# Causal attention and a gated linear unit on one core: every engine's queue ordered by a list schedule written into the kernel, the first batch loaded pair by pair

## The chip, the cores and the metric

The kernel runs on one core of a Trainium2 chip. A core has five instruction queues that run beside each other and wait for one another on semaphores: PE (matrix products and transposes), DVE (vector work), ACT (exponentials, tanh, copies), POOL (a slower vector engine) and SP (which here only issues DMA transfers). The metric is the device time of one execution in microseconds. Three runs of the kernel before took 287.56, 288.27 and 291.65 us, median 288.27.

## What is computed

```
scores = q @ k.T / 8                      # 8 batches, 8 heads, 576 positions, 64 wide
cum    = cumsum(max(s, 0))                # per head, over positions
scores = causal(scores + min(cum[key] - cum[query], 0))
x      = softmax(scores) @ v              # heads side by side: 576 x 512 per batch
gate   = sigmoid(sum over 5 shifts of conv_w[k] * shifted x)    # per channel
out    = (gate * (x @ w_val)) @ w_out
```

The causal mask makes the decay a product of a factor of the query and a factor of the key, so the kernel multiplies the key's factor into v once (the tile `Vp`) instead of adding a bias to every score. A ones column beside v gives the softmax's sum.

## The kernel before

The unit of work is a **pair**: two heads of one batch, 32 pairs in all, four to a batch. For each batch:

- SP loads q and k (`load_qk`, L260, 1 MB each), the last 64 positions of both (`tail`, L268) and v (`load_v`, L330, five blocks into the one buffer `vst`).
- POOL converts q, k and tail to bf16 (L262, L270) and multiplies v by the decay factor `w` (L332, five instructions). For batch 0 alone the conversions are DVE's.
- PE transposes tail (L343) and, per pair, q and k (L353, 8 transposes); ACT copies the results out of PSUM into `QKT` (L344, L354).

For each pair: three groups of score products (L359, masks added by L396) with an exponential on ACT after each (L397); 30 products with `Vp` into the one PSUM buffer `psav` (`av`, L409); a reciprocal and a multiply on DVE (L417, L418, "norm"); five transposes of the result on PE (L429) and a copy to `xT` on DVE (L430); the convolution on DVE as five instructions per pair, "taps" (L437 the first, L439 the other four); tanh on ACT (L441). For each batch then eight products with w_val (`val`, L451), each with a DVE multiply by the gate (L453, "glu"), and five products with w_out (`outp`, L461), each with a copy on ACT (L464) and a store (L465). A short check of the reciprocals on DVE (L552 to L555) ends in a count that every engine reads.

Score groups take turns on two PSUM buffers; transposes, val, outp and the conversion of conv_w (L488, L489, to the tile `cwT` that all taps read) share two more, `m`.

What sets the order: `fills(n)` lists the work besides the scores that pair n brings (the next batch's transposes among it), half of the waiting list is emitted after every two score groups, and the build's own scheduler then moves instructions within each queue. At the start w_val and w_out are loaded after v, and POOL converts them (L481).

## Time and profile before

| | us |
|---|---|
| three runs | 287.56, 288.27, 291.65 |
| the profiled execution | 286.0 |
| its span, first to last instruction | 284.2 |
| DVE busy | 215.8 (76%) |
| PE busy | 208.3 (73%) |
| ACT busy | 175.5 (62%) |
| POOL busy | 108.6 (38%) |

The busy shares are means over a span with different limits. At the start the engines wait for the first loads and conversions, in the middle DVE is busy nearly all the time, and at the end PE and ACT finish the last two batches' products while DVE has little left. "Busy" counts the time in which at least one instruction of the engine was under way. A wait is put down to the event that came last.

### The profile page before, as it was taken

How to read it: one execution, taken by the hardware profiler on the slowest of the kernel's cores; microseconds unless marked ns; L12 is line 12 of the kernel's file. 1: busy time of each engine (PE TensorE's matmuls, PEld its weight loads, DVE VectorE, ACT ScalarE, POOL GpSimd, SP SyncE). 2: the span in 40 equal slices, each digit the busy share in tenths (PEclk: the TensorE clock that was granted, in tenths of full speed). 3: DMA queues.
4: the chain of work that ended last, by engine and by line, in shares of the span. 5: the costliest groups of instructions: out<-in, count | busy, mean ns of one | idle time of the engine just before them, and what ended most of it. 6: DMA issues, size and time to landing. Idle time of an engine off the chain costs nothing. (4 is left out here: it accounts for less than half of the span.)

```text
span 284.2 us, 6148 instructions
## 1 busy us (share of the span) xinstructions
PE 208.3 (73%) x2534; PEld 135.4 (48%) x2555; DVE 215.8 (76%) x342; ACT 175.5 (62%) x218; POOL 108.6 (38%) x87
## 2 busy tenths in 40 slices
PE   0779285468859977587878967798689898774990
PEld 0547263247534744464555634564366556442540
DVE  4303229997999799949997799949995999999310
ACT  1389264756564867587648866795659887622250
POOL 9379976940691046602490229201810000000000
PEclk9999869567995999999959999999989999997996
DMA  6997999999410029955868486501100201210342
GB/s 171 292 293 234 256 261 240 273 241 281 115 38 0 2 88 246 267 88 131 258 201 174 120 267 157 127 21 74 40 37 17 80 37 40 92 39 37 129 161 76
DMA packets 69054, 40.49 MB, mean 142 GB/s; under 512 B 46933, under 2 KB 63317, under 8 KB 69018
## 3 DMA queue, kind: packets, MB, share of 16 engines
q1 hardware_dynamic: 69018, 40.01, 52.6%
q8 instruction: 22, 0.36, 0.6%
q14 instruction: 14, 0.11, 0.1%
HBM read 30.57 MB, written 9.44 MB: 141 GB/s over the span
## 5 line engine op out<-in xcount | busy, mean ns | idle before, releaser
L439 DVE SCALAR_TENSOR_TENSOR gp<-xT,cwT,gp 128x576 f32<-128x576 bf16 x128 | 126.2, 992 | 0.6
L397 ACT ACTIVATE P<-ps 128x1024 bf16<-128x1024 f32 x96 | 94.5, 1024 | 19.8 <-PE ps L359 11.2
L332 POOL TENSOR_TENSOR Vp<-vst,w 128x520 bf16<-128x520 f32 x40 | 55.2, 1405 | 31.6 <-PE psav L409 25.9
L359 PE MATMUL ps<-QKT 64*128 64x128 bf16 (+4 forms) x576 | 49.3, 259 | 16.7 <-ACT P L397 15.1
L409 PE MATMUL psav<-Vp,P 128*128 128x65 bf16 x960 | 45.0, 201 | 11.1 <-DVE xn L418 10.9
L262 POOL CAST qkb<-qkf 128x2048 bf16<-128x2048 f32 x14 | 28.6, 2046 | 58.1 <-PE m L353 27.2
L409 PEld LDWEIGHTS <-P 128*128 128x128 bf16 x960 | 38.5, 102 | 22.4 <-issue 16.7
L461 PE MATMUL m<-wo,glu 128*128 128x512 bf16 x139 | 40.2, 396 | 11.7 <-DVE glu L453 9.5
L451 PE MATMUL m<-xT,wv 128*128 128x288 bf16 x256 | 41.3, 299 | 9.0 <-ACT ot L464 6.3
L441 ACT ACTIVATE th<-gp 128x576 f32<-128x576 f32 x32 | 21.9, 686 | 34.5 <-DVE gp L439 34.1
L359 PEld LDWEIGHTS <-QKT 64*128 64x128 bf16 x576 | 23.6, 99 | 39.0 <-issue 31.5
L464 ACT COPY ot<-m 128x512 f32<-128x512 f32 (+1 forms) x40 | 23.3, 582 | 22.8 <-PE m L461 10.6
L354 ACT COPY QKT<-m 128x1024 bf16<-128x1024 bf16 x32 | 31.4, 1019 | 5.6 <-PE m L353 5.6
L451 PEld LDWEIGHTS <-wv 128*128 128x128 bf16 x256 | 24.1, 101 | 21.6 <-issue 15.1
L453 DVE SCALAR_TENSOR_TENSOR glu<-th,m 128x288 bf16<-128x288 f32 x64 | 28.6, 447 | 5.5 <-PE m L451 5.5
L430 DVE COPY xT<-m 128x576 bf16<-128x576 bf16 x32 | 14.5, 452 | 24.0 <-PE m L429 23.0
L461 PEld LDWEIGHTS <-glu 128*128 128x128 bf16 x160 | 15.5, 99 | 27.1 <-issue 14.6
L353 PE MATMUL m<-ident,qkb 128*128 128x128 bf16 x256 | 22.5, 244 | 5.5 <-ACT QKT L344 2.5
L418 DVE TENSOR_TENSOR xn<-psav,recs 128x640 bf16<-128x640 f32 x32 | 26.2, 818 | 0.3
L437 DVE TENSOR_SCALAR gp<-xT,cwT 128x576 f32<-128x576 bf16 x32 | 24.7, 771 | 1.8
L353 PEld LDWEIGHTS <-qkb 128*128 128x128 bf16 x256 | 18.9, 110 | 9.0 <-issue 6.6
L417 DVE RECIPROCAL recs<-psav 128x10 f32<-128x10 f32 x32 | 6.8, 212 | 15.9 <-PE psav L409 15.9
(52 smaller groups left out, 118.2 us busy)
## 6 DMA issues: line engine op xcount, KB each, us to landing
vst<-in_v_dram SPq DMA_DIRECT2D x32, 256.0 KB, 5.5
out_dram<-ot SPq DMA_DIRECT2D x32, 256.0 KB, 2.0
qkf<-in_q_dram SPq DMA_DIRECT2D x7, 1024.0 KB, 6.8
qkf<-in_k_dram SPq DMA_DIRECT2D x7, 1024.0 KB, 8.5
tail<-in_q_dram SPq DMA_DIRECT2D x8, 128.0 KB, 7.8
tail<-in_k_dram SPq DMA_DIRECT2D x8, 128.0 KB, 6.9
vst<-in_v_dram SPq DMA_DIRECT2D x8, 128.0 KB, 5.0
qkf<-in_moe_w_val_dram SPq DMA_DIRECT2D x1, 1024.0 KB, 6.5
```

The source lines that it names most:

```text
L262: cast(t.rearrange("p j (h d) -> p h j d", h=8)[:, h0:h1], f.rearrange("p h (j d) -> p h j d", j=4)[:, h0:h1])
L332: nc.gpsimd.tensor_tensor(Vp[:, i], vst[:, i], w[:, i, b * 8:(b + 1) * 8].unsqueeze(2).to_broadcast([128, 8, 65]), ALU.mult)
L353: nc.tensor.transpose(pt[:, which, j * 128:(j + 1) * 128], st["qk"][which][:, j, c], ident)
L354: nc.scalar.copy(st["QKT"][:, :, p, 0:512].rearrange("d w (x j) -> d w x j", j=4), pt.rearrange("d w (j x) -> d w x j", j=4))
L359: nc.tensor.matmul(ps[:, hh, c0:c0 + nq], st["QKT"][r, 1, p, k0:k0 + 128], st["QKT"][r, 0, p, q0:q0 + nq], **kw)
L397: nc.scalar.activation(out=st["P", p][:, :, step * 512:(step + 1) * 512], in_=ps, func=AF.Exp, scale=0.125)
L409: nc.tensor.matmul(psav[:, hh, qb * 65:qb * 65 + 65], lhsT, Vp[:, kb, 2 * p + hh, :], start=(kb == 0), stop=(kb == qb))
L418: nc.vector.tensor_tensor(st["xn"][:, :, p * 128:(p + 1) * 128].rearrange("t g (h d) -> t h g d", h=2), pv[:, :, :, 0:64], rec.unsqueeze(3 ...
L439: nc.vector.scalar_tensor_tensor(gp, xc[:, kk:kk + S], cwT[:, c, kk:kk + 1], gp, ALU.mult, ALU.add)
L451: nc.tensor.matmul(psv, wv[:, dc, c * 128:(c + 1) * 128], st["xT"][:, dc, 4 + o:4 + o + 288], start=(dc == 0), stop=(dc == 3))
L453: nc.vector.scalar_tensor_tensor(st["glu"][:, c, o:o + 288], st["th", c][:, o:o + 288], 1.0, psv, ALU.add, ALU.mult)
L461: nc.tensor.matmul(pso, st["glu"][:, c, WIN[i]:WIN[i] + 128], wo[:, c, :], start=(c == 0), stop=(c == 3))
```

## The change

Nothing that is computed changes, and nearly every instruction exists before and after in the same shape. What the change does:

- **Order.** The kernel's code first lists every piece of work as a task with an engine, a cost, a due time (the table `DUE`, relative to the pair's number), the tasks it depends on and the buffers it takes and gives. `Plan.run` then steps through time and gives each free engine the ready task with the earliest due time. The tasks are emitted in that order, and the build's scheduler is told to keep it.
- **First batch.** q and k of batch 0 come pair by pair into their own buffers instead of two parts; v of batch 0 in twelve transfers (two per pair of 128 KB and one of 32 KB) instead of five. The conversion of k is ACT's (four of 128x512), that of q DVE's (four of 128x512). The four multiplications of v by the decay factor are DVE's.
- **Weights.** w_val and w_out are converted by DVE instead of POOL, and are loaded after q and k of batch 1, w_out later than those of batch 2.
- **v of later batches.** POOL multiplies by pair (four instructions of 128x650) instead of by block (five of 128x520).
- **Buffers.** Each buffer is one tile with one name; the plan gives out the numbers. There are six `th` buffers instead of five, and q's and k's bf16 tiles have two each instead of three in common.

```diff
+DUE = dict(av=1.09, norm=1.14, xt=0.4, xe=-1.97, tap=1.69, dtap=0.24, tanh=1.19, cpe=-13.67, val=4.62,
+           dval=0.22, out=9.31, dout=0.72, oute=4.54, qt=-4.04, qe=-3.19, tt=-2.41, te=-5.83, s4=-0.87,
+           vp=-4.81, cast=-10.12, lqk=-10.71, lv=4.53)
...
+            for e in engs:
+                if idle_at[e] > now + 1e-9:
+                    nxt.append(idle_at[e])
+                    continue
+                pick = None
+                seen = 0
+                for t in todo[e]:
+                    at = ready_at(t)
+                    seen += 1
+                    if seen > 60:
+                        break
+                    if at is None:
+                        continue
+                    if at > now + 1e-9:
+                        nxt.append(at)
+                        continue
...
+    t_wvo = []
+    for nm, src, dst, sc, key in (("wv", moe_w_val, wv, 1.0, -5), ("wo", moe_w_out, wo, 0.5, -2.4)):
+        def load(nm=nm, src=src):
+            wt = slot[nm] = work("qkf", nm, [128, 4, DM], FP32)
+            nc.sync.dma_start(out=wt, in_=src.rearrange("(c p) d -> p c d", c=4))
+        t = add("SP", 3.6, key, load, take=[("qkf", nm)])
+        t_wvo.append(add("DVE", 1.35, key + 7, lambda nm=nm, dst=dst, sc=sc: nc.vector.tensor_scalar(
+            dst, slot[nm], sc, None, ALU.mult), [t], give=[("qkf", nm)]))
+    t_wv, t_wo = t_wvo
...
+    t = add("SP", 0.3, -1, lambda: nc.sync.dma_start(out=cw, in_=moe_conv_w))
+    t = add("PE", 0.3, 0, conv_T, [t], take=[("m", "cw")], mode="N")
+    t_cw = add("DVE", 0.15, 0.1, lambda: nc.vector.tensor_copy(cwT, slot["cw"]), [t], give=[("m", "cw")])
...
+    def vprime(eng, b, p):
+        h = slice(2 * p, 2 * p + 2)
+        eng.tensor_tensor(Vps[b % 2][:, :, h], vst[:, :, h],
+                          w[:, :, b * 8 + 2 * p:b * 8 + 2 * p + 2].unsqueeze(3).to_broadcast([128, NKB, 2, 65]),
+                          ALU.mult)
+
+    def load_v_pair(p):
+        for h in (2 * p, 2 * p + 1):
+            nc.sync.dma_start(out=vst[:, 0:4, h, 0:64], in_=v[0, h, 0:512, :].rearrange("(i p) d -> p i d", i=4))
+        nc.sync.dma_start(out=vst[64:128, 4, HP[p], 0:64],
+                          in_=v[0, HP[p], 512:576, :].rearrange("h s d -> s h d"))
...
-    def load_v(b):
...
-            nc.gpsimd.tensor_tensor(Vp[:, i], vst[:, i],
...
+            t_tl = add("SP", 1.6, -8.4, lambda: load_tail(0))
+            t_tail = T["tailc", 0] = add("DVE", 0.45, -6, lambda: nc.vector.tensor_copy(tailbs[0], tails[0]), [t_tl])
+            for p in range(4):
+                for wh in range(2):
+                    def ld(p=p, wh=wh):
+                        f = slot["f", 0, wh, p] = one.tile([128, 2, 256], FP32, name=f"first{p}{wh}")
+                        dma_qk(0, wh, HP[p], f)
+                    t = add("SP", 0.95, -8.5 + 0.5 * p + wh * 0.01, ld)
+                    T["cast", 0, wh, p] = add(("DVE", "ACT")[wh], (0.32, 0.5)[wh], p - 9, lambda p=p, wh=wh: cast_qk(
+                        (nc.vector.tensor_copy, nc.scalar.copy)[wh], 0, wh, HP[p], slot["f", 0, wh, p]), [t])
+                t = add("SP", 1.4, -8.3 + 0.5 * p, lambda p=p: load_v_pair(p))
+                T["vp", 0, p] = add("DVE", 0.85, p - 2, lambda p=p: vprime(nc.vector, 0, p), [t, t_w])
...
+                t = add("SP", 3.8, n0 + DUE["lqk"], ld, take=[("qkf", (b, wh))])
+                c = add("POOL", 1.95, n0 + DUE["cast"], lambda b=b, wh=wh: cast_qk(
+                    nc.gpsimd.tensor_copy, b, wh, slice(0, 8), slot["f", b, wh]),
+                    [t] + [T.get(("qt", b - 2, p)) for p in range(4)], give=[("qkf", (b, wh))])
...
+                T["vp", b, p] = add("POOL", 1.4, n0 + p + DUE["vp"], lambda b=b, p=p: vprime(nc.gpsimd, b, p),
+                                    ts + [t_w, T.get(("av", b - 2, p))])
...
-        nc.gpsimd.tensor_scalar(dst, wt, sc, None, ALU.mult)
...
+    plan.total = plan.run()
+    with tc.manual_schedule():
+        for t in plan.order:
+            t["emit"]()
```

The start on DVE, from the first batch's last two norms to the first tap (`psav` and `xn` are the norm, `xT` the copy after PE's transposes, `cwT` the convolution's weights, `gp` the taps). Before:

```order
L418 TENSOR_TENSOR xn<-psav,recs 128x2x5x64
L489 COPY cwT<-m 128x20
L417 RECIPROCAL recs<-psav 128x10
L418 TENSOR_TENSOR xn<-psav,recs 128x2x5x64
L417 RECIPROCAL recs<-psav 128x10
L418 TENSOR_TENSOR xn<-psav,recs 128x2x5x64
L430 COPY xT<-m 128x576
L437 TENSOR_SCALAR gp<-xT,cwT 128x576
L439 SCALAR_TENSOR_TENSOR gp<-xT,cwT,gp 128x576
```

and with the change:

```order
L599 TENSOR_TENSOR xn_116<-psav,recs 128x2x5x64
L611 COPY xT_118<-m_502 128x576
L598 RECIPROCAL recs<-psav 128x10
L599 TENSOR_TENSOR xn_116<-psav,recs 128x2x5x64
L454 TENSOR_SCALAR wv<-qkf_176 128x2048
L477 COPY cwT<-m_614 128x20
L618 TENSOR_SCALAR gp_628<-xT_118,cwT 128x576
L611 COPY xT_118<-m_622 128x576
L621 SCALAR_TENSOR_TENSOR gp_628<-xT_118,cwT,gp_628 128x576 x4
```

The conversion of w_val (`wv`) now stands between the last norm of batch 0 and the copy that makes `cwT`, and three of batch 0's four copies to `xT` have moved ahead of it; before, all of them stood behind the four norms.

On PE the weights of the convolution are transposed from `cw`. With the change, behind the first two score groups of batch 1 (`QKT_113` is batch 1's, `xn_116` holds the norms of batch 0):

```order
L537 MATMUL s_607<-QKT_113 128x448
L537 LDWEIGHTS QKT_113
L537 MATMUL s_607<-QKT_113 128x448
L461 MATMUL m_614<-identf,cw 128x5 x4
L607 LDWEIGHTS xn_116
L607 MATMUL m_622<-ident,xn_116 128x128
L607 LDWEIGHTS xn_116
```

Before, that transposition stood between two products of batch 0 with `Vp`:

```order
L409 MATMUL psav<-Vp_162,P 128x65
L409 LDWEIGHTS P
L409 MATMUL psav<-Vp_162,P 128x65
L488 MATMUL m<-identf,cw 128x5 x4
L409 LDWEIGHTS P
L409 MATMUL psav<-Vp_162,P 128x65
L409 LDWEIGHTS P
```

So it moved from batch 0's attention to behind batch 1's transposes and two of its score groups.

The end on DVE: glu are the multiplies by the gate, `ok` and `okm` the check. Before:

```order
L439 SCALAR_TENSOR_TENSOR gp<-xT,cwT,gp 128x576 x4
L453 SCALAR_TENSOR_TENSOR glu<-th,m 128x288
L439 SCALAR_TENSOR_TENSOR gp<-xT,cwT,gp 128x576
L453 SCALAR_TENSOR_TENSOR glu<-th,m 128x288
L439 SCALAR_TENSOR_TENSOR gp<-xT,cwT,gp 128x576
L552 TENSOR_SCALAR ok<-recs 128x320
L553 SCALAR_TENSOR_TENSOR ok<-recs,ok 128x320
L555 TENSOR_REDUCE okm<-ok 128x1
L453 SCALAR_TENSOR_TENSOR glu<-th,m 128x288 x8
L560 CAST okcnt<-m 1x1
```

With the change:

```order
L621 SCALAR_TENSOR_TENSOR gp_3777<-xT_119,cwT,gp_3777 128x576
L651 SCALAR_TENSOR_TENSOR glu_121<-th_3725,m_3799 128x288
L651 SCALAR_TENSOR_TENSOR glu_121<-th_3779,m_3805 128x288
L621 SCALAR_TENSOR_TENSOR gp_3777<-xT_119,cwT,gp_3777 128x576
L651 SCALAR_TENSOR_TENSOR glu_121<-th_3779,m_3812 128x288
L790 TENSOR_SCALAR ok<-recs 128x320
L791 SCALAR_TENSOR_TENSOR ok<-recs,ok 128x320
L792 TENSOR_REDUCE okm<-ok 128x1
L651 SCALAR_TENSOR_TENSOR glu_121<-th_3824,m_3818 128x288
L651 SCALAR_TENSOR_TENSOR glu_121<-th_3824,m_3830 128x288
L800 CAST okcnt<-m_3858 1x1
```

Before, eight glu stand behind the last tap and the check; with the change three stand behind the last tap, two of them behind the check.

## Rows read from the trace of the kernel before

**Rows 1.** Windows: length; PE, PEld, DVE, ACT, POOL busy us; clock, DMA share, GB/s.
```profile
0.00:41.00 41.00, 24.40 (x302) 17.35 (x302) 11.06 (x21) 21.67 (x24) 33.33 (x39) 0.92 0.93 247
...
41.00:261.60 220.60, 169.90 (x2163) 110.92 (x2181) 199.74 (x311) 146.70 (x182) 75.24 (x49) 0.93 0.48 126
...
261.60:284.20 22.60, 14.04 (x73) 7.15 (x73) 4.97 (x13) 7.11 (x12) 0.00 (x0) 0.88 0.34 115
...
219.00:239.00 20.00, 17.77 (x246) 11.35 (x249) 19.15 (x35) 15.89 (x20) 0.00 (x0) 1.00 0.17 61
```

**Rows 2.** DVE's longest waits between 41.0 and 261.6: total us, times, longest.
```profile
DVE xT L430 <- PE m L429: 23.0, 7, 8.1
```

**Rows 3.** Timeline of the start: start us, duration us, engine, line, operation, what ended the wait.
```profile
20.89 5.37 POOL L481 TENSOR_SCALAR wv<-qkf 128x2048 bf16<-128x2048 f32 x1 [1.31 <-DMA qkf<-in_moe_w_val_dram]
...
31.57 3.72 POOL L262 CAST qkb<-qkf 128x2048 bf16<-128x2048 f32 x2
...
35.24 0.61 POOL L270 CAST tailb<-tail 128x512 bf16<-128x512 f32 x1
...
41.04 0.86 DVE L437 TENSOR_SCALAR gp<-xT,cwT 128x576 f32<-128x576 bf16 x1
```

**Rows 4.** Windows of the first 20 us: the last column is GB/s.
```profile
0.00:10.00 10.00, 1.72 (x15) 1.53 (x16) 4.34 (x10) 2.09 (x3) 8.52 (x24) 1.00 0.75 224
10.00:20.00 10.00, 7.80 (x73) 4.68 (x72) 1.91 (x2) 7.17 (x9) 5.28 (x5) 1.00 1.09 263
```

**Rows 5.** Timeline of the start: prices of loads, casts and evacuations.
```profile
2.49 0.68 SPq L268 DMA_DIRECT2D tail<-in_q_dram  x1
...
5.30 8.96 SPq L330 DMA_DIRECT2D vst<-in_v_dram  x5
...
12.30 0.96 DVE L262 CAST qkb<-qkf 128x1536 bf16<-128x1536 f32 x1 [1.35 <-DMA qkf<-in_k_dram]
...
27.82 0.41 PE L488 MATMUL m<-identf,cw 5*128 5x5 f32 x4
...
36.55 0.58 ACT L344 COPY QKT<-m 128x512 bf16<-128x512 bf16 x1 [6.28 <-PE m L343]
...
37.41 1.93 ACT L354 COPY QKT<-m 128x1024 bf16<-128x1024 bf16 x2 [0.27 <-PE m L353]
```

**Rows 6.** Timeline of DVE beside POOL (43 to 58 us) and without it (229 us).
```profile
43.47 2.12 POOL L262 CAST qkb<-qkf 128x2048 bf16<-128x2048 f32 x1 [1.89 <-PE ps L371]
...
43.76 2.15 DVE L437 TENSOR_SCALAR gp<-xT,cwT 128x576 f32<-128x576 bf16 x1
...
50.16 7.37 POOL L332 TENSOR_TENSOR Vp<-vst,w 128x520 bf16<-128x520 f32 x5
...
51.09 1.24 DVE L439 SCALAR_TENSOR_TENSOR gp<-xT,cwT,gp 128x576 f32<-128x576 bf16 x1
...
229.05 0.51 DVE L437 TENSOR_SCALAR gp<-xT,cwT 128x576 f32<-128x576 bf16 x1
...
229.61 0.81 DVE L439 SCALAR_TENSOR_TENSOR gp<-xT,cwT,gp 128x576 f32<-128x576 bf16 x1
```

**Rows 7.** POOL's groups between 41.0 and 261.6: busy us, mean ns of one.
```profile
L332 POOL TENSOR_TENSOR Vp<-vst,w 128x520 bf16<-128x520 f32 x31 | 45.8, 1507 | 25.9 <-PE psav L409 25.9
```

**Rows 8.** Timeline of the end: cold matmuls, the last tap, its tanh, the first glu.
```profile
259.90 1.87 PE L461 MATMUL m<-wo,glu 128*128 128x512 bf16 x4 [3.44 <-DVE glu L453]
...
260.86 0.81 DVE L439 SCALAR_TENSOR_TENSOR gp<-xT,cwT,gp 128x576 f32<-128x576 bf16 x1
...
261.70 0.68 ACT L441 ACTIVATE th<-gp 128x576 f32<-128x576 f32 x1 [2.23 <-DVE gp L439]
...
262.87 0.45 DVE L453 SCALAR_TENSOR_TENSOR glu<-th,m 128x288 bf16<-128x288 f32 x1
```

**Rows 9.** The chain that ended last: start us, duration us, what.
```profile
266.79 0.88 PE m L461 x4
...
276.89 0.58 ACT ot L464
```

More of the change, by code (lines that the diff above doesn't have):

```diff
@@ L311, in main_path @@
[L311 to L321 removed]
+    P4s = [one.tile([128, 2, 4, 128], BF16, name=f"P4{j}") for j in range(2)]
@@ new lines, in main_path @@
+    for P4 in P4s:
+        nc.gpsimd.memset(P4[:, :, :, 0:64], 0.0)
+    two = lambda name, shape, dt: [one.tile(shape, dt, name=f"{name}{j}") for j in range(2)]
+    qkbs = [two("qb", [128, 4, 512], BF16), two("kb", [128, 4, 512], BF16)]
+    tails, tailbs = two("tail", [128, 512], FP32), two("tailb", [128, 512], BF16)
+    QKTs = two("QKT", [128, 2, 4, S], BF16)
+    Vps = two("Vp", [128, NKB, 8, 65], BF16)
+    xns = two("xn", [128, NKB, 512], BF16)
+    xTs = two("xT", [128, 4, 4 + S], BF16)
@@ L338, in tail_transpose @@
[L338 to L350 removed]
+    t = add("DVE", 0.65, -8, relu, [t_s])
@@ L563 @@
+    t = add("DVE", 1.3, NS + 6, check_recs, [T["norm", n] for n in range(NS)])
+    t = add("PE", 0.2, NS + 6.1, count, [t], take=[("m", "c")], mode="N")
+    add("DVE", 0.1, NS + 6.2, lambda: nc.vector.tensor_copy(okcnt, slot["c"]), [t], give=[("m", "c")])
+    plan.total = plan.run()
+    with tc.manual_schedule():
+        for t in plan.order:
+            t["emit"]()
+    return plan
 @with_exitstack
```

612 lines of the change are left out of this document (370 added, 242 removed).

## The prediction

> **What bounds the kernel now.** I read the windows first. The span of 284.2 us falls into three parts [rows 1]. Until the first tap at 41.04 us [rows 3] DVE is busy for 11.06 of 41.0 us: the start waits for loads and conversions. From there to the last tap it is busy for 199.74 of 220.6 us: the middle is DVE's. In the last 22.6 us DVE has 4.97 us of work, and PE and ACT drain the products. In the middle DVE's waits name one culprit: 23.0 us stand at the copy to `xT`, waiting for PE's transposes, 8.1 of them in one piece that ends just ahead of the first tap [rows 2]. That leaves 14.9 us of such waits in the middle; 220.6 - 199.7 - 14.9 = 6.0 us are small gaps between instructions.
>
> The middle is not all work at DVE's own speed. A tap takes 0.81 us alone and 1.24 us beside POOL's multiplication of v [rows 6]. The change leaves POOL's work for the later batches in place, so this tax stays.
>
> So the time is: first tap + DVE's work + its waits and gaps + tail + what lies outside the span. The profiled execution took 286.0 us with its 284.2 us span, so 1.8 us lie outside; it is 0.8% under the median of the three runs, 288.27.
>
> **The start.** The first tap now comes late because POOL converts w_val from 20.89 us on for 5.37 us, and w_out behind it, before batch 1's q and k at 31.57; `tail` is done at 35.85, and only behind that does ACT copy batch 1's transposes (36.55, after a wait of 6.28) and PE come to `xT` [rows 3, 5]. The change takes both weights off POOL. What is late next is batch 1's q, k and tail themselves: on PE the transposition of `cw` stands behind batch 1's transposes and two of its score groups, and on DVE every tap needs `cwT`.
>
> I count bytes from the shapes. Ahead of and with batch 1's k: s 0.15, q and k 2.10, tails 0.26, v 1.18, q and k again 2.10, in all 5.79 MB; with batch 1's tails 6.05; with w_val 7.10. At 224 and 263 GB/s, 4.87 MB are there by 20 us [rows 4], and at 263 GB/s 5.79 MB by 23.5, 6.05 by 24.5, 7.10 by 28.5. The same count for w_val before (4.74 MB) gives 19.5, and POOL began on it at 20.89 [rows 3], so I add 1.4 us: k at 24.9, tails at 25.9, w_val at 29.9. POOL's conversion of k takes 1.86 (half of 3.72), so it ends at 26.8, that of tail 0.61, so 27.4 [rows 3]. ACT then copies four pairs and the tail, 4 x 0.97 + 0.58 = 4.5 us [rows 5], to 32.0; PE's score groups lie beside them. Transposing `cw` takes 0.41 us [rows 5], with the copy some 0.9: **first tap at 33**. DVE's conversion of w_val, 2048 columns at the price of 0.96 us for 1536 [rows 5], takes 1.28 and ends at 31.2, hidden under that chain by 1.8 us; without that cover the excess goes to the first tap. Lower bound: if batch 1 were no obstacle, w_val's landing at the plain byte count and its conversion, 30. Upper bound: no gain, 41.
>
> The rest of the start costs nothing that I can see. Twelve v transfers for five: five took 8.96 us to issue, 1.8 each for 256 KB, and a 128 KB one 0.68 [rows 5]; eight at 0.68 and four smaller ones at no more make 8.2, the same again. DVE's four multiplications of v (no row has them; 650 columns against a tap's 576 at 0.81 [rows 6], so between 0.8 and 1.4, POOL's price of a fifth more of them, and I take 0.9) lie in DVE's 29.9 idle us of the first 41 [rows 1]; so do four conversions of q. k's four conversions on ACT, at the 0.58 of a 512-column copy [rows 5], are 2.3 us, on an engine busy for 21.7 of those 41 us [rows 1].
>
> **The middle.** DVE's work: 199.7. The order shows three `xT` copies before the first tap that were behind it (-3 x 0.45), five more glu before the last tap (+5 x 0.45, the price of one [rows 8]), and w_out's conversion (+1.3, as w_val's). POOL's multiplication of batch 1's v, now lies beside taps altogether; before, one of its five blocks did (31 in the middle are 30 and that one [rows 7]). 4 x 1.51 us [rows 7] at (1.24 - 0.81)/1.24 = 0.35 us of DVE per us of POOL [rows 6], +2.1. Sum 204.0; bounds 201.9, if that costs nothing, and 207.9, if DVE loses all the 6.0 us that POOL works. The 6.0 us of gaps stay.
>
> The waits for transposes, 14.9 us now, are what the new order is to remove: with it the transposes of the next batch are spread over pairs and most `xT` copies stand a norm behind their own. But the order also sets two norms back to back here and there, with one `psav` between them. Bounds 0 and 14.9; I take 5, a third, since the mechanism goes but some of its places stay.
>
> Here a row speaks against one part of the change. A first tap, one tensor and a scalar, takes 0.51 us alone and 2.15 us when it meets POOL's conversion of 2.12 us [rows 6]. The Trainium skill (Advanced Engine Details and Errata, VectorE Performance Modes) says that Vector's second SBUF port is shared with GPSIMD, so that GPSIMD instructions and two-port Vector instructions block each other; that fits the rows. By it the two weight conversions moved to DVE could each wait out a POOL instruction, some 2 us each: w_val's would lie within a fraction of a microsecond of its cover, w_out's would be paid, and the sum would be about 2 us higher.
>
> **The tail.** After the last tap (260.86 + 0.81 = 261.67) the chain is tanh 0.68 (it began 0.03 behind) and the check's 1.2 us, which still stands ahead of the last two glu (261.67 to 262.87) [rows 8]. With it three glu instead of eight remain, 3 x 0.45, so the last is done some 2.5 us behind the tap. Six outp follow from about 2.1, one of them batch 6's, at 0.88 [rows 9]: 5.3. The count needs one of the two `m` buffers between them, 0.5, the last copy 0.6, and from that copy's end (277.47 [rows 9]) to 284.2 it is 6.7 us now. Sum 2.1 + 5.3 + 0.5 + 0.6 + 6.7 = 15.2 against 22.6. If PE is cold, as it was after waiting for 3.44 us, an outp takes 1.87 [rows 8], 6 x 0.99 = 5.9 more: 21.1. PE still has val and outp of two batches there, so I take **16**, near the warm end.
>
> **Sum.** 33 + 204 + 6 + 5 + 16 = 264 us of span, 266 with the 1.8 outside; against 286.0, -7%. The gain is 8 us at the start, 10 in the middle's waits less 4 of added work, and 6.6 in the tail.
>
> **Rivals.**
> - *All waits go.* First tap 30, middle 204 + 6, tail 15: 255 + 1.8 = 257. For it: DVE was busy 19.15 of 20 us where POOL was quiet [rows 1]. Against: back-to-back norms remain.
> - *PE becomes the bound.* In the same stretch PE was busy 17.77 of 20 us at full clock [rows 1]. If the middle stays at 220.6 us because PE, not DVE, paces it: 33 + 220.6 + 16 + 1.8 = 271. Against: PE has 169.9 us of work in the middle [rows 1], and at 17.77 in 20 that is 191 us, under DVE's 204.
> - *The start doesn't move.* `cwT` behind batch 1 is a new dependence in queue order; if it keeps the first tap at 41: 274.
> - *Nothing moves.* The order brings no fewer waits, the start stays and the tail is cold: 41 + 204 + 6 + 14.9 + 21 + 1.8 = 289, within 2% of now.
> - *Slower: POOL's queue holds v back.* With a fixed queue, the conversion of a later batch's q can stand ahead of this batch's four multiplications of v, and it waits for its load and for a free bf16 tile; `av`, its norm and DVE wait behind it. It is paid once for each of the batches 2 to 7. My 20 us of gain are gone at 3.3 us a batch, and it is slower by 2% at 4.3. At the longest wait seen, 8.1 us [rows 2], it would be 6 x 8.1 less the 5 us assumed: 310. Against: POOL is busy for 75 of 220.6 us [rows 1], and a batch's `av` are four pairs apart.
>
> **How the numbers follow.** The forecast 0.56 (own range 259 to 275), all waits go 0.12, PE the bound 0.10, the start doesn't move 0.07, nothing moves 0.08, slower 0.07. The first four end under 282.5, so faster by over 2%, about what a measurement of this kernel can tell from no change, has 0.85, within 2% 0.08, slower 0.07. The range 253 to 280 takes in the four and leaves out the last two and a little of the edges.
>
> **What would show it.** Right: the first tap near 33 us, started by `cwT`; waits of DVE for `xT` under 8 us; three glu behind the last tap and a tail near 16 us. Wrong: DVE's busy time in the middle well off 204 (the tax of POOL misjudged), waits at the norm in the place of those at `xT`, or PE busy for over 90% there.

## The result, and the profile after

The changed kernel takes 278.27 us (median of four runs, 278.12 to 278.72) against 287.91 for the kernel before: a ratio of 0.971, 95% interval 0.962 to 0.980. It is faster by 3%, where 7% was forecast. Executions of one kernel mostly agree within 3% here; a profile shows one of them, and the tables say how long that one took.

The windows of the profiled execution after (278.2 us), which answer to [rows 1]. The columns are window, length, busy us of PE, PEld, DVE, ACT and POOL, TensorE's granted clock, DMA share, GB/s:

```profile
0.00:33.50 33.50, 21.55 (x328) 15.71 (x329) 15.46 (x29) 24.99 (x33) 12.86 (x28) 0.95 0.97 242
33.50:262.10 228.60, 172.30 (x2183) 112.77 (x2203) 213.79 (x308) 146.90 (x186) 74.55 (x45) 0.87 0.52 136
262.10:276.30 14.20, 6.33 (x30) 2.69 (x29) 2.44 (x7) 4.18 (x7) 0.00 (x0) 0.85 0.30 99
```

| | before | forecast | after |
|---|---|---|---|
| first tap | 41.0 | 33 | 33.5 |
| first to last tap ("the middle") | 220.6 | 215 | 228.6 |
| DVE busy in it | 199.7 | 204 | 213.8 |
| DVE idle in it | 20.9 | 11 | 14.8 |
| behind the last tap | 22.6 | 16 | 14.2 |

The start gains 7.5 us and the tail 8.4, close to the 8 and 6.6 of the forecast. The whole miss stands in the middle: it was to shrink by 6 us and grew by 8. It is DVE that grew, by 14.1 us of busy time, while its idle time fell by 6.

The start after, on DVE (answers to [rows 3]):

```profile
30.94 1.23 DVE L454 TENSOR_SCALAR wv<-qkf 128x2048 bf16<-128x2048 f32 x1 [1.38 <-DMA qkf<-in_moe_w_val_dram]
33.26 0.18 DVE L477 COPY cwT<-m 128x20 f32<-128x20 f32 x1 [1.09 <-PE m L461]
33.47 0.52 DVE L618 TENSOR_SCALAR gp<-xT,cwT 128x576 f32<-128x576 bf16 x1
```

DVE's waits in the middle (engine, line, what it waited for: total us, times, longest), which answer to [rows 2]:

```profile
DVE recs L598 <- PE psav L592: 5.2, 4, 2.8
DVE glu L651 <- PE m L645: 3.2, 7, 1.0
...
DVE xT L611 <- PE m L607: 1.0, 3, 0.6
```

and, in the kernel before, those that stand beside the waits at `xT`:

```profile
DVE recs L417 <- PE psav L409: 2.3, 3, 1.1
DVE xT L430 <- PE psav L409: 0.7, 1, 0.7
DVE glu L453 <- PE m L451: 0.2, 1, 0.2
```

The waits for transposes are gone, 1.0 us in place of 14.9; norms and glu wait instead. DVE's groups in the middle, before and then after (busy us, in which overlapping instructions count once, mean ns | idle ahead of them):

```profile
L439 DVE SCALAR_TENSOR_TENSOR gp<-xT,cwT,gp 128x576 f32<-128x576 bf16 x128 | 126.2, 992 | 0.6
L453 DVE SCALAR_TENSOR_TENSOR glu<-th,m 128x288 bf16<-128x288 f32 x56 | 25.0, 446 | 0.2 <-PE m L451 0.2
L437 DVE TENSOR_SCALAR gp<-xT,cwT 128x576 f32<-128x576 bf16 x32 | 24.7, 771 | 1.8
```

```profile
L621 DVE SCALAR_TENSOR_TENSOR gp<-xT,cwT,gp 128x576 f32<-128x576 bf16 x128 | 131.6, 1028 | 2.7
L651 DVE SCALAR_TENSOR_TENSOR glu<-th,m 128x288 bf16<-128x288 f32 x62 | 26.9, 447 | 3.6 <-PE m L645 3.2
L618 DVE TENSOR_SCALAR gp<-xT,cwT 128x576 f32<-128x576 bf16 x32 | 24.0, 750 | 1.4
...
L454 DVE TENSOR_SCALAR wo<-qkf 128x2048 bf16<-128x2048 f32 x1 | 2.4, 2447 | 0.0
```

The recorded times of all DVE instructions between the start of the first tap and the end of the last add up to 219.9 us before and 227.5 after, 7.6 more. But busy time grew by 14.0 between these points. The other 6.4 us are overlap that was lost: a DVE instruction's recorded time runs on after the next has begun, by 219.9 - 199.8 = 20.1 us in all before, and by only 227.5 - 213.8 = 13.7 after. What overlaps, and what does not, stands in the timelines. First the kernel before, around one norm, then the kernel after, from its first taps and from the place where POOL converts q and k and multiplies v:

```profile
132.78 0.21 DVE L417 RECIPROCAL recs<-psav 128x10 f32<-128x10 f32 x1
132.91 0.80 DVE L439 SCALAR_TENSOR_TENSOR gp<-xT,cwT,gp 128x576 f32<-128x576 bf16 x1
133.62 0.82 DVE L418 TENSOR_TENSOR xn<-psav,recs 128x640 bf16<-128x640 f32 x1
134.36 0.45 DVE L430 COPY xT<-m 128x576 bf16<-128x576 bf16 x1
```

```profile
34.38 3.37 DVE L621 SCALAR_TENSOR_TENSOR gp<-xT,cwT,gp 128x576 f32<-128x576 bf16 x4
...
130.30 3.17 DVE L621 SCALAR_TENSOR_TENSOR gp<-xT,cwT,gp 128x576 f32<-128x576 bf16 x2
133.40 2.14 DVE L618 TENSOR_SCALAR gp<-xT,cwT 128x576 f32<-128x576 bf16 x1
135.57 1.72 DVE L621 SCALAR_TENSOR_TENSOR gp<-xT,cwT,gp 128x576 f32<-128x576 bf16 x1
137.21 0.21 DVE L598 RECIPROCAL recs<-psav 128x10 f32<-128x10 f32 x1
137.45 0.82 DVE L599 TENSOR_TENSOR xn<-psav,recs 128x640 bf16<-128x640 f32 x1
138.19 4.36 DVE L621 SCALAR_TENSOR_TENSOR gp<-xT,cwT,gp 128x576 f32<-128x576 bf16 x3
...
130.95 1.92 POOL L489 CAST qb<-qkf 128x2048 bf16<-128x2048 f32 x1 [7.16 <-issue]
132.81 2.41 POOL L489 CAST kb<-qkf 128x2048 bf16<-128x2048 f32 x1
135.19 6.74 POOL L499 TENSOR_TENSOR Vp<-vst,w 128x650 bf16<-128x650 f32 x4
```

Before, a tap of another chunk stands between a norm's reciprocal and its multiplication; the tap starts 0.13 us behind the reciprocal and the multiplication 0.71 behind the tap, so each begins before the one ahead has ended. After, the multiplication needs the reciprocal just ahead and starts 0.24 behind it. The four taps of one chunk, each of which needs the one before, take 3.37 us: (3.37 - 0.81)/3 = 0.85 us from start to start. Over all pairs of the middle that POOL leaves alone, a tap with a dependent one behind it takes 0.849 us to the next start (36 of them after), one with an independent one 0.733 (56). **Theory A** of the experiments: such dependent neighbours, 21 in the middle before and 104 after (25 and 108 in the whole queue, counted in the traces; the recorded expectations have 27 for 25), cost about 0.115 us each: 83 x 0.115 = 9.5 us. Lost overlap of 6.4 us, and small gaps of 5.4 us in place of 2.8 (idle time less the named waits, those of over 0.15 us), make 9.1. **Theory B**: taps in a row meet POOL more. **Theory C**: TensorE, at a granted clock of 0.87 in the middle in place of 0.93, is late.

### The profile page after: what moved, and what is told of

Its sections match the earlier page's. It is cut to its first block, busy times and chain, and to the rows that moved or that the text cites. A ratio compares the mean times of both kernels' runs of the same rounds, so it can differ in the third digit from the quotient of the medians.

```text
span 276.3 us, 6143 instructions
## 1 busy us (share of the span) xinstructions
PE 200.2 (72%) x2540; PEld 131.2 (47%) x2561; DVE 231.7 (84%) x342; ACT 176.1 (64%) x225; POOL 87.4 (32%) x73
## 4 chain that ended last, share of the span: by engine, by line
DVE 71%; PE 16%; ACT 5%; issue 4%; DMA 1%; DVEq 0%; ACTq 0%
DVE gp L621 42%; DVE gp L618 8%; DVE xn L599 7%; DVE glu L651 7%; DVE xT L611 4%; PE m L645 4%; PE m L657 3%; PE psav L592 3%; ACT P L582 3%; PE m L528 2%; PE s L537 2%; ACT QKT L532 2%; DVE recs L598 1%; DMA sp<-in_s_dram 1%; DVE wo L454 1%
## 5 line engine op out<-in xcount | busy, mean ns | idle before, releaser
L621 DVE SCALAR_TENSOR_TENSOR gp<-xT,cwT,gp 128x576 f32<-128x576 bf16 x128 | 131.6, 1028 | 2.7
L582 ACT ACTIVATE P<-s 128x1024 bf16<-128x1024 f32 x96 | 95.4, 1029 | 26.0 <-PE s L537 13.8
L499 POOL TENSOR_TENSOR Vp<-vst,w 128x650 bf16<-128x650 f32 x28 | 45.1, 1638 | 37.4 <-DMA vst<-in_v_dram 23.6
L645 PE MATMUL m<-xT,wv 128*128 128x288 bf16 x256 | 44.7, 314 | 13.1 <-DVE glu L651 8.5
L537 PE MATMUL s<-QKT 64*128 64x128 bf16 (+4 forms) x576 | 42.7, 262 | 9.6 <-ACT P L582 7.4
L592 PE MATMUL psav<-Vp,P 128*128 128x65 bf16 x960 | 38.6, 202 | 10.5 <-DVE xn L599 10.5
L592 PEld LDWEIGHTS <-P 128*128 128x128 bf16 x960 | 36.5, 103 | 15.3 <-issue 8.9
L625 ACT ACTIVATE th<-gp 128x576 f32<-128x576 f32 x32 | 22.0, 686 | 30.4 <-DVE gp L621 30.3
L532 ACT COPY QKT<-m 128x1024 bf16<-128x1024 bf16 x32 | 32.2, 1014 | 13.7 <-PE m L528 13.6
L662 ACT COPY ot<-m 128x512 f32<-128x512 f32 (+1 forms) x40 | 23.5, 587 | 14.2 <-PE m L657 9.1
L651 DVE SCALAR_TENSOR_TENSOR glu<-th,m 128x288 bf16<-128x288 f32 x64 | 27.7, 447 | 3.6 <-PE m L645 3.2
L489 POOL CAST qb<-qkf 128x2048 bf16<-128x2048 f32 x7 | 14.1, 2016 | 43.9 <-PE m L528 17.9
L528 PE MATMUL m<-ident,qb 128*128 128x128 bf16 x128 | 13.9, 238 | 16.8 <-DVE chalf L431 6.1
L607 PE MATMUL m<-ident,xn 128*128 128x128 bf16 x160 | 15.8, 235 | 12.3 <-DVE xn L599 5.5
L657 PEld LDWEIGHTS <-glu 128*128 128x128 bf16 x160 | 14.7, 99 | 20.9 <-issue 9.7
L697 POOL CAST tailb<-tail 128x512 bf16<-128x512 f32 x7 | 5.9, 850 | 45.4 <-PE m L517 33.2
L607 PEld LDWEIGHTS <-xn 128*128 128x128 bf16 x160 | 11.2, 105 | 19.0 <-DVE xn L599 13.3
```

The lines of the kernel that those rows point to most:

```text
L499: eng.tensor_tensor(Vps[b % 2][:, :, h], vst[:, :, h], w[:, :, b * 8 + 2 * p:b * 8 + 2 * p + 2].unsqueeze(3).to_broadcast([128, NKB, 2, 65 ...
L532: nc.scalar.copy(QKTs[b % 2][:, :, p, 0:512].rearrange("d w (x j) -> d w x j", j=4), slot["qt", b, p].rearrange("d w (j x) -> d w x j", j=4))
L537: nc.tensor.matmul(ps[:, hh, c0:c0 + nq], QKTs[b % 2][r, 1, p, k0:k0 + 128], QKTs[b % 2][r, 0, p, q0:q0 + nq], **kw)
L582: nc.scalar.activation(out=slot["Pt", n][:, :, step * 512:(step + 1) * 512], in_=slot["s", n, step], func=AF.Exp, scale=0.125)
L592: nc.tensor.matmul(psav[:, hh, qb * 65:qb * 65 + 65], lhsT, Vps[b % 2][:, kb, 2 * p + hh, :], start=(kb == 0), stop=(kb == qb))
L607: nc.tensor.transpose(pt[:, WIN[i]:WIN[i] + 128], xns[b % 2][:, i, p * 128:(p + 1) * 128], ident)
```

## The experiments

"Neighbours" are pairs in DVE's queue of which the second needs the first, counting taps and norms. Times are medians; "profiled" is the execution that was profiled, and the columns right of it are read in it (middle, busy and idle are DVE's).

| run | us | ratio to before | profiled | first tap | middle | busy | idle | tail | neighbours |
|---|---|---|---|---|---|---|---|---|---|
| before | 287.9 | | 286.0 | 41.0 | 220.6 | 199.7 | 20.9 | 22.6 | 25 |
| after | 278.3 | 0.971 | 278.2 | 33.5 | 228.6 | 213.8 | 14.8 | 14.2 | 108 |
| e1_apart | 280.5 | 0.982 | 276.1 | 34.6 | 223.1 | 206.9 | 16.2 | 16.5 | 60 |
| e2_alternate | 276.5 | 0.963 | 278.3 | 35.1 | 226.1 | 210.7 | 15.4 | 15.2 | 49 |
| order_undone_2 | 270.6 | 0.943 | 270.0 | 33.7 | 221.0 | 207.9 | 13.1 | 13.5 | 60 |
| dve_order_undone | 275.6 | 0.957 | 276.7 | 35.1 | 226.2 | 211.2 | 15.0 | 13.5 | 60 |
| true_costs_apart | 271.8 | 0.945 | 274.6 | 35.2 | 224.4 | 207.0 | 17.4 | 13.1 | 22 |
| swaps_taps_only | 279.3 | 0.971 | 280.4 | 34.4 | 229.6 | 212.6 | 17.0 | 14.5 | 82 |
| swaps_norm_only | 277.0 | 0.963 | 276.5 | 34.7 | 225.7 | 210.4 | 15.3 | 14.2 | 70 |
| first_taps_act_apart | 276.6 | 0.967 | 275.9 | 36.4 | 219.4 | 194.6 | 24.8 | 18.0 | 67 |
| b_start | 286.9 | 0.994 | 286.1 | 39.7 | 220.5 | 200.5 | 20.0 | 24.0 | 25 |
| b_start_loads | 286.4 | 0.998 | 288.2 | 38.2 | 223.5 | 202.1 | 21.5 | 24.8 | 26 |

Theory A can be checked in all of these orders at once. The next table has what overlap and small gaps give back against the changed kernel, and beside it the two things that move with the order as well: what taps and weight conversions lose beside POOL (their time above 0.81, 0.52 and 1.25 us), and the named waits.

| run | neighbours fewer, middle | at 0.115 us each | overlap and gaps give | lost beside POOL | named waits |
|---|---|---|---|---|---|
| after | 0 | 0 | 0 | 36.2 | 9.4 |
| before | 83 | 9.5 | 9.1 | 31.4 | 18.1 |
| e1_apart | 48 | 5.5 | 4.9 | 32.8 | 12.1 |
| e2_alternate | 59 | 6.8 | 7.5 | 36.9 | 12.8 |
| order_undone_2 | 48 | 5.5 | 5.8 | 34.0 | 9.5 |
| dve_order_undone | 48 | 5.5 | 4.8 | 35.7 | 11.1 |
| true_costs_apart | 86 | 9.9 | 11.2 | 36.9 | 16.0 |
| swaps_taps_only | 26 | 3.0 | 3.2 | 36.9 | 13.0 |
| swaps_norm_only | 36 | 4.1 | 4.5 | 36.6 | 11.6 |

So what a neighbour costs comes back every time, within 1.3 us. Whether the time follows depends on the last two columns, on the start and on the tail. Each row is one execution.

### POOL's work taken away, after and before

```diff
     def vprime(eng, b, p):
         h = slice(2 * p, 2 * p + 2)
+        if b > 1:
+            return
...
     def cast_qk(eng, b, which, hs, f):
+        if b > 1:
+            return
```

> The changed kernel with POOL's work left out from batch 2 on: no conversion of q, k and tails and no multiplication of v there, and q, k and tails of these batches aren't loaded; the tiles keep what batches 0 and 1 put there, so the results of batches 2 to 7 are those of other data. DVE's order is unchanged. It sizes POOL's tax: the taps and first taps that lie beside POOL are 34 us longer together than alone, 6/7 of that is 29, so DVE is busy for some 185 us in the middle instead of 213.9. Theory B (the growth over the kernel before is POOL's): DVE's busy time falls to that of the kernel before without POOL's work, within 3 us. Theory A: it stays 7 to 10 us above it, since 108 dependent neighbours are still there.

> The kernel before with the same work left out (POOL's conversions and multiplications from batch 2 on, the loads of q, k and tails). The taps beside POOL are 31 us longer together than alone; without 6/7 of that, DVE is busy for some 174 us in the middle instead of 199.7. Theory A wants the difference of the two kernels to remain at 7 to 10 us of the 14.1, theory B at 3 or less.

244.35 and 253.35 us, one run each. The middle after, then before:

```profile
34.60:228.10 193.50, 160.59 (x2203) 106.14 (x2203) 180.64 (x308) 145.80 (x187) 6.54 (x4) 0.96 0.34 85
```

```profile
40.40:228.00 187.60, 161.61 (x2182) 105.41 (x2181) 168.99 (x310) 145.97 (x183) 0.87 (x1) 0.98 0.29 74
```

The work left out costs DVE 33.2 us after and 30.8 before, 2.4 of the 14.1 us by which DVE grew. A little of POOL's work stays, and more of it after (6.54 us for 0.87: batch 1's v), beside which taps lose 3.6 us for 0.7. With that, POOL's share of the growth is some 5 us, as 36.2 against 31.4 in the table above, and some 9 are there without POOL: theory B falls as the main cause. And the middle gives back all of it, 35.1 us for 33.2 of DVE: with every queue in its order, it follows DVE's time. TensorE's granted clock rose too, from 0.87 to 0.96, so these runs don't set theory C aside.

### Neighbours kept apart in the plan

```diff
+                    if e == "DVE":
+                        if last is not None and last in t["deps"]:
+                            second = second or t
+                            continue
+                        if second is None or t["key"] <= second["key"] + 1.2:
+                            pick = t
+                        break
...
+            t = add("DVE", 0.14, n + DUE["norm"], lambda n=n: recip(n), [t])
+            t = T["norm", n] = add("DVE", 0.74, n + DUE["norm"], lambda n=n: norm(n), ...
```

> The changed kernel, but its list schedule, when it picks DVE's next instruction, passes over one that needs the result of the one just issued if another is ready; and the reciprocal and the multiplication of a norm are two tasks, so that something can stand between. Neighbours of which the second needs the first (tap after tap of one chunk, reciprocal then multiplication): 60 in place of 108 (27 in the kernel before). Theory A (such a pair costs: a tap's start to the next start is 0.85 us where the next needs it and 0.73 where it doesn't): 48 x 0.115 = 5.5 us less in the middle, DVE's busy time there some 210, time about 273. Theory B (POOL's instructions hold DVE longer because taps stand in a row): taps still follow taps, 81 neighbours for 92, so under 1 us less. Theory C (TensorE's lower granted clock, 0.87 against 0.93 in the middle, makes PE late and DVE waits for it): DVE's order changes nothing, time 278 within 1, and what DVE gains it waits.

> As the run with dependent neighbours kept apart, and the list schedule also prefers, after a tap, a ready instruction that isn't a tap (a norm's part, glu, a copy to xT) and the other way round, from up to six pairs ahead. Neighbours that need each other: 49 for 108. Tap next to tap: 58 for 92 (41 in the kernel before). Theory A: 59 x 0.115 = 6.8 us less, time about 271. Theory B: a tap beside POOL waits 0.9 us for POOL's multiplication, but 0.45 where a glu stands between, so of the 4 us by which the tax grew, some 2.7 come back on top: 269. Both alone: A without B 271.5, B without A 275.5. Theory C: 278 within 1. A cost of its own: glu that wait for a tap hold PE's two buffers longer, up to 8 glu a batch by half a tap, which would show as PE waiting for DVE at m.

With 48 neighbours fewer, e1_apart's middle is 5.5 us shorter in the profiled execution (276.06 us, the shortest of the four), and start and tail give 3.4 back. That theory A had just these 5.5 is in part luck: overlap and gaps give 4.9, POOL takes 3.4 less, and named waits take 2.7 more. Its four times run from 276.06 to 283.33, ratio 0.982 (0.968 to 0.996), so its time settles nothing. e2_alternate's middle, in the longest of its four executions, is 2.5 us shorter for 59 neighbours, where 6.8 were expected: overlap and gaps give 7.5, but named waits take 3.5 more. Its ratio of 0.963 (0.951 to 0.975) can't be told from the changed kernel's. With 58 taps next to taps in place of 92, the taps and the weight conversion that lie beside POOL still last 36.9 us longer than they would at 0.81, 0.52 and 1.25 us alone (36.2 in the changed kernel): theory B falls here too.

### The order given back to the build

```diff
-    with tc.manual_schedule():
+    if True:
         for t in plan.order:
             t["emit"]()
```

> The changed kernel, but the planned order isn't kept: the build orders the queues itself, as it does for the kernel before, from the same instructions and buffers. Neighbours on DVE that need each other: 60 in place of 108. Theory A: DVE's busy time in the middle falls by 44 x 0.08 = 3.5 us or more, to 210; whether the time falls too depends on its waits, 9.4 us in pieces over 0.15 us with the fixed order; if these go back to the kernel before's 18, it is 278 - 3.5 + 9 = 283. Rival W (the fixed order is what costs, waits included): time under 274. Theory C (TensorE's clock): nothing in DVE's busy time changes.

> The kernel of the run before in which the build orders the queues, once more, for a profile of an execution near its median of 270 us. Theory A with waits as they are: first tap at 33 to 34, DVE's busy time in the middle 207 to 211 with 56 dependent neighbours where the fixed order has 104, tail 13 to 15. Of the 8 us to the changed kernel, then, 48 x 0.115 = 5.5 us are dependent neighbours, and the rest must stand in DVE's waits or POOL's tax. Rival W: its DVE is as busy as in the changed kernel, 212 to 214, and all 8 us are waits.

270.21 us, ratio 0.941 (0.935 to 0.946), and again 270.64, 0.943 (0.934 to 0.953): 8 us less than with the fixed order, from the same instructions and buffers. The middle, its waits, and the first taps of the profiled execution (270.03 us):

```profile
33.70:254.70 221.00, 172.93 (x2203) 110.96 (x2203) 207.89 (x310) 146.47 (x186) 78.65 (x46) 0.92 0.54 141
```

```profile
DVE glu L651 <- PE m L645: 3.7, 5, 1.3
DVE recs L598 <- PE psav L592: 3.1, 4, 1.2
DVE xT L611 <- PE m L607: 2.4, 7, 0.6
```

```profile
35.11 5.91 DVE L621 SCALAR_TENSOR_TENSOR gp<-xT,cwT,gp 128x576 f32<-128x576 bf16 x8
```

Eight taps of two chunks in turn take 5.91 us: (5.91 - 0.81)/7 = 0.73 from start to start, where the fixed order's four of one chunk have 0.85. The middle is 7.6 us shorter, 5.9 of that DVE's busy time. The waits come to 9.2 us, 9.4 in the changed kernel: nearly nothing of the 8 us is there, and rival W of the second run falls. The time of the first run had gone the way of its rival W (under 274) and not of theory A's 283, which reckoned that the kernel before's waits would come back. The groups of DVE:

```profile
L621 DVE SCALAR_TENSOR_TENSOR gp<-xT,cwT,gp 128x576 f32<-128x576 bf16 x128 | 129.6, 1022 | 1.7
...
L618 DVE TENSOR_SCALAR gp<-xT,cwT 128x576 f32<-128x576 bf16 x32 | 22.7, 710 | 1.6 <-ACT th L625 0.3
```

Taps and first taps last 2.1 us less (their means times their counts), all of it beside POOL. All instructions together last 225.4 us, so 17.6 overlap in place of 13.7: 3.9 us. Small gaps are 3.6 us for 5.4. For the 48 neighbours that is 5.8 us, where 5.5 were reckoned, and with the taps 7.9 for the 7.6.

### Only DVE's queue changed

dve_order_undone keeps the planned queues of PE, ACT, POOL and SP and takes DVE's queue from the run above, 123 of 342 places differ:

```diff
+    todo["DVE"] = [todo["DVE"][i] for i in DVE_ORDER]
```

The three swap runs keep the planned queues too and let neighbours change places with the instruction behind them, all (39 neighbours left), only taps (82), or only a norm's multiplication (70):

```diff
+        if d[i - 1] in d[i]["deps"] and d[i - 1] not in d[i + 1]["deps"] and not needs(d[i + 1], d[i]) \
+                and d[i] not in d[i + 2]["deps"]:
+            d[i], d[i + 1] = d[i + 1], d[i]
```

> The changed kernel; the queues of PE, ACT, POOL and SP are exactly as planned, and only DVE's queue is that which the build made in the run with the order undone: the same instructions, 123 of 342 places differ. Theory A (DVE's own queue holds the loss): time 270 to 273, DVE's busy time 207 to 211. Rival W (the fixed order loses in how PE's and ACT's queues meet DVE's): time 277 to 281, since a DVE queue made for another PE queue waits more.

> The changed kernel with the queues of PE, ACT, POOL and SP exactly as planned; in DVE's queue, wherever an instruction needs the result of the one ahead and the next but one doesn't, those two change places (reciprocal and multiplication of a norm counting as two). No instruction moves by more than a place or two; 39 dependent neighbours stand where 108 did, 69 taps next to taps where 92 did. Theory A: 69 x 0.115 = 7.9 us less in the middle, DVE's busy time there 213.8 - 69 x 0.08 = 208 or less, time 270 to 272 if at most 2 us go into waits. Theory B: POOL's tax falls too, from 36 to about 34 us, time 268 to 270. Theory W (the middle is paced by how PE's and ACT's queues meet DVE's, not by DVE's own time): DVE's busy time falls but its waits grow by as much, time 277 to 279.

> As the run with planned swaps, but each norm stays whole (reciprocal, then at once its multiplication) in its place; only a tap that needs the one ahead changes places with the instruction behind it. 82 dependent neighbours for 108; psav is held 1.07 us as in the changed kernel. If dependent neighbours alone count: 26 x 0.115 = 3.0 us less, DVE busy 211 to 212, waits for psav at about 5 us as in the changed kernel, time 275 to 276. If any change of DVE's queue against the planned PE queue makes waits: busy 211 to 212, waits of 14 us or more, time 278 to 280.

> As the run with planned swaps, but only the norms' swaps: between a reciprocal and its multiplication stands one tap or glu. 70 dependent neighbours for 108 (reciprocal then multiplication 3 for 32). By dependent neighbours alone: 38 x 0.115 = 4.4 us less, time 274. If the longer hold on psav is what costs: waits for psav grow from 5 to 11 us or more in the middle, and the time is 277 to 281.

dve_order_undone takes 275.61 us, ratio 0.957 (0.948 to 0.967): a third of the 8 us, between what theory A and rival W had, and not quite clear of the changed kernel's 0.962 to 0.980. DVE's queue is that of order_undone_2, yet between their profiled executions lie 6.6 us. Taps and first taps last 2.8 us longer, all of it beside POOL, DVE idles 2.0 us more, and the first tap comes 1.4 us later. planned_swaps took 275.92 to 280.61, median 279.68, ratio 0.960 (0.949 to 0.971). Its profiled execution (280.32) has DVE busy for 211.0 us and 17.5 us of named waits, nearer to theory W than to theory A's 270 to 272. Its two halves were then run one by one. The middle of swaps_taps_only and its longest waits, then the middle of swaps_norm_only:

```profile
34.40:264.00 229.60, 172.35 (x2183) 113.42 (x2203) 212.56 (x308) 147.04 (x187) 74.94 (x45) 0.88 0.50 133
```

```profile
DVE glu L686 <- PE m L680: 6.1, 8, 1.7
DVE recs L629 <- PE psav L624: 5.2, 4, 2.0
```

```profile
34.70:260.40 225.70, 170.41 (x2183) 111.09 (x2203) 210.37 (x308) 146.69 (x186) 75.86 (x45) 0.89 0.52 136
```

Parting the norms takes 3.4 us off DVE's busy time, as 38 x 0.08 = 3.0 says, and the middle follows (-2.9); the longer hold on `psav`, 1.78 us for 1.07, didn't bring the longer waits that were feared (4.0 us at the norm, 5.2 in the changed kernel). The start gives 1.2 of it back, and the time, 277.02, with a ratio of 0.963 (0.952 to 0.973), isn't clear of the changed kernel's. Parting taps takes 1.2 us off, and glu that now come one place earlier wait 6.1 us for val in place of 3.2: nothing is left, and the time is the changed kernel's, ratio 0.971 (0.961 to 0.982). So neighbours cost what the rows say in DVE's time, but in front of the queues planned for the old places part of the gain turns into waits for PE and into time lost beside POOL. The reverse, DVE's queue as planned and PE's and ACT's as the build made them, wasn't run.

### The plan with measured costs

```diff
-                    t = add("DVE", 0.5 if m == 0 else 0.78, ...
+                    t = add("DVE", 0.8 if m == 0 else 1.03, ...
...
-                T["vp", b, p] = add("POOL", 1.4, ...
+                T["vp", b, p] = add("POOL", 1.64, ...
```

> The changed kernel, with the planner's costs for DVE and POOL set to the means measured in its profile (a tap 1.03 us for 0.78, a first tap 0.8 for 0.5, POOL's multiplication 1.64 for 1.4), and dependent neighbours kept apart as in the first experiment, the norm in two tasks. The plan now finds something else to issue nearly always: 22 dependent neighbours in place of 108 (27 before), 63 taps next to taps for 92. Theory A: 86 x 0.115 = 9.9 us less of DVE in the middle, busy time 204 or less, time 268 if the waits stay, 272 if they grow by 4 as in the first experiment. Theory B: nearly 30 pairs of taps fewer, so POOL's tax falls from 36 to 34 us on top. Theory C: time unchanged.

> The kernel of the run with the measured costs in the plan, dependent neighbours kept apart and the norm in two tasks, but the planned order only sets the order in which instructions are written, and the build orders the queues, as in the run with the order undone. 57 dependent neighbours, as there (60). Theory A, by DVE's own time: 270 as in the run with the order undone, within 2. If a plan with true costs also leaves the build a better order of PE and ACT: 265 to 268. Theory W: waits decide, and no sum over DVE's rows gives the time; anything from 266 to 276.

true_costs_apart, with neighbours kept apart as well, takes 271.78 us, ratio 0.945 (0.936 to 0.954): a fixed order that plans all queues for DVE's true speed has 6.5 us of the 8. The row in the table is of its longest execution (274.6 us). There overlap and gaps give 11.2 us, and named waits take 6.6 more. Written out by that plan but ordered by the build, undone_true_costs takes 278.40, ratio 0.960 (0.951 to 0.970), with 57 neighbours and DVE busy for 208.6 us of a middle of 231.5: its 22.9 idle us decide. All three expectations ended at or under 276. What helps one ordering doesn't add to the other.

### First taps on ACT

```diff
-            nc.vector.tensor_scalar(gp, xc[:, 4:4 + S], cwT[:, c, 4:5], None, ALU.mult)
+            nc.scalar.activation(out=gp, in_=xc[:, 4:4 + S], func=AF.Copy, scale=cwT[:, c, 4:5])
```

> The changed kernel with the first tap of each of the 32 chunks (one tensor and a scalar) on ACT, as a copy with a scale per partition, instead of DVE; the plan then fixes an order for that. It asks whether DVE's work bounds the middle. These first taps take DVE 24.6 us of starts to next starts, 7.5 of it waited out beside POOL. Theory A (the middle is DVE's work): DVE's busy time falls to 190 to 198, part of POOL's tax moving to the next tap, and the time to 260 to 267, with waits as they are; with waits 5 us longer, 265 to 272. Theory C (PE, late at its lower clock, paces the middle): DVE waits for what it no longer works, time 275 to 279. ACT gets 32 x 0.68 = 22 us on top of 147 of 229.

> As the run with the first taps on ACT, and dependent neighbours kept apart as in the first experiment, with the norm in two tasks: 67 such neighbours in place of 94. Theory A: 27 x 0.115 = 3.1 us less of DVE than in that run, and the time 0 to 3 us lower, as waits have it. Rival: with DVE relieved this far, PE and ACT pace the middle, DVE's busy time falls by 2 and its waits grow by as much, time the same within 1.

first_taps_act took 280.13 to 289.65 us, median 288.67, slower than the changed kernel. With neighbours apart it is 276.58, ratio 0.967 (0.962 to 0.971). The waits of the latter in the middle:

```profile
DVE recs L608 <- PE psav L603: 11.0, 12, 2.7
DVE gp L635 <- ACT gp L632: 6.0, 6, 1.6
```

DVE has 19.2 us less to do and idles 10 us more: a tap waits for ACT's first tap, and the norm waits for PE's `av`, the products that need ACT's exponentials, and in ACT's queue the first taps now stand among these. The start and the tail lose 6.7. My "waits as they are" was wrong. By its time alone theory C (275 to 279) would do as well for the second run; the granted clock in its middle is 0.90, above the changed kernel's 0.87, and which of the two makes PE late wasn't run.

### The new start alone

```diff
-        nc.gpsimd.tensor_scalar(dst, wt, sc, None, ALU.mult)
+        nc.vector.tensor_scalar(dst, wt, sc, None, ALU.mult)
```

with batch 0 in four pairs, on the kernel before; b_start_loads also has batch 1's loads ahead of w_val's and w_out's load a batch later.

> The kernel before with the change's start alone: w_val and w_out converted on DVE instead of POOL, batch 0's q and k in four pairs (k's conversion on ACT), batch 0's v in twelve transfers and multiplied by pair on DVE. The order of everything else is still found by the build. Theory A (the start and the tail bring what was forecast, the fixed order's loss lies in DVE's middle): first tap at 33 to 35 instead of 41.0, DVE's busy time from the first to the last tap as before, 200 within 2 (w_out's conversion falls before the first tap in this order), its waits there still 15 to 20, the tail still 22 to 23: time 286 - 7 = 279, the same as the changed kernel within 3. Rival S (the start's gain needs the fixed order too): first tap still at 39 to 41, time 286 within 2.

> The kernel before with the change's start, and now also its order of loads: batch 1's q, k and tails ahead of w_val, and w_out's load and conversion a batch later. With the weights still ahead of batch 1, POOL got q at 28.4, k at 32.1 and tail at 33.9, and the first tap stayed at 39.7. Theory L (the order of the loads, not POOL's conversions, is what the start's gain hangs on): POOL has k at 25 to 26, tail done by 28.5, ACT's five copies 4.5 us, first tap at 33 to 35, time 286 - 6 = 280. Rival S (PE's fixed order is needed too): first tap at 37 to 40, time 285 to 288.

Ratios 0.994 (0.989 to 0.999) and 0.998 (0.992 to 1.003): no gain worth the name. In b_start, POOL, free of the weights, waits for the loads behind them:

```profile
28.42 1.89 POOL L262 CAST qkb<-qkf 128x2048 bf16<-128x2048 f32 x1 [19.58 <-DMA qkf<-in_q_dram]
32.06 1.90 POOL L262 CAST qkb<-qkf 128x2048 bf16<-128x2048 f32 x1 [1.74 <-DVE xn L429]
33.90 0.62 POOL L270 CAST tailb<-tail 128x512 bf16<-128x512 f32 x1
```

In b_start_loads POOL has tail done at 30.4, but the build put `cwT`'s copy behind w_val's conversion on DVE, and that holds the `m` buffer that PE needs for batch 1's transposes; PE's transposes of x stand behind those:

```profile
33.47 1.87 PE L364 MATMUL m<-ident,qkb 128*128 128x128 bf16 x16 [2.60 <-DVE cwT L504]
```

```profile
33.25 0.17 DVE L504 COPY cwT<-m 128x20 f32<-128x20 f32 x1
37.66 0.46 DVE L441 COPY xT<-m 128x576 bf16<-128x576 bf16 x1 [4.24 <-PE m L440]
```

So the 7.5 us of the start come from three things at once: the weights off POOL, their loads behind batch 1's, and a PE queue in which neither batch 1's transposes wait for `cwT` nor those of x stand behind all of them. The third is read from these timelines; no run changed it alone.

## Why the prediction was right or wrong

- **The start**: right (33.5 for 33), and by the chain that was forecast: POOL was done with k at 27.7 us and with tail at 28.3, 0.9 later than reckoned, and `cw` was transposed from 32.8 on. Its story of the kernel before was too short: it named POOL's conversions as what holds the first tap. The runs on the kernel before show that taking only these away, and then also the order of loads, leaves it at 39.7 and 38.2. The order on PE and DVE, which the forecast took from the changed queues without naming it a cause, is needed too.
- **The tail**: right (14.2; the sum had 15.2, the forecast took 16). Three glu stand behind the last tap.
- **The waits**: too low by some 4 us, 14.8 idle for 11. Those at `xT` went, 14.9 to 1.0 us; norms and glu took 8.4, where 5 us in all were assumed beside the gaps. The "6.0 us of gaps" were misread: 3.2 of them were waits for `psav` and val, and 2.8 small gaps. "Waits at the norm in the place of those at xT" was named as a thing that could go wrong and did, in 5.2 us.
- **DVE's work in the middle: the step that failed.** "DVE's work: 199.7", with a few instructions added and taken, carried a busy time from one order to another as if it belonged to the instructions. It belongs to the order: 20.1 us of it was saved by overlap, and the new order has 13.7, since 104 instructions stand right behind the one they need where 21 did. Busy time came to 213.8 for 204. Of the 9.8 us, 6.4 are lost overlap, 1.8 are taps beside POOL (taps and first taps last 3.9 longer, forecast 2.1), 1.1 is w_out's conversion (2.45 us for 1.3), and smaller items make 0.5. The same neighbours make 2.6 us more of small gaps, which "the 6.0 us of gaps stay" missed. The prediction had named a busy time well off 204 as a sign of being wrong, with POOL's tax as the reason; the sign came, the reason is the smaller part of it. The order view that stands ahead of the forecast shows one such place, at the start: four taps of one `gp` in a row.
- **w_out's conversion**: the rule of the Trainium skill (Advanced Engine Details and Errata, VectorE Performance Modes) that was weighed and not taken came true where it was to cost: 2.45 us beside POOL against 1.23 for w_val, beside which POOL had nothing under way. That is 1.2 us, where some 2 were reckoned.
- **The rivals**: none was it. "The start doesn't move" (274) is nearest in time, but the start moved; "PE becomes the bound" (271) comes next, but PE was busy for 172 of 228.6 us. That its lower clock made part of the miss isn't excluded: order_undone_2 has 0.92 in the middle, the changed kernel 0.87, and no run changed the clock alone. But late PE shows in DVE's waits: 9.4 us in the middle, fewer than the 18.1 before, so it can't be why the middle grew, and against order_undone_2 they are the same within 0.2 us.
- **Open**: why DVE's queue alone brings back only a third of what reordering all queues does. Where the rest goes shows in the profiles (taps beside POOL, waits for PE, a later first tap; in the swap runs glu before val is done). How much of this each of the other queues makes, no run shows.

## What to carry to other kernels

A busy time is not a property of the instructions: before carrying it over to another order, count how many neighbours on the bounding engine need each other, and price both kinds by their distance from start to start. A list schedule that knows neither this nor what another engine's work adds to an instruction (here a tap beside POOL) plans for a DVE that doesn't exist; here giving it measured means and letting it part neighbours, or leaving the order to the build, beat it by 6.5 and 8 us, and both together by nothing. Price a change of the start with all that stands ahead of it, loads and queue places included, not with the one engine seen busy.
